# Loading Q, K and V of one batch ahead of a weight, and moving its attention steps, in a fused attention and mixer kernel

## The chip, the core and the metric

The kernel runs on one core of one Trainium2 chip. The metric is the device time of one execution in microseconds (us). Six executions of the kernel before took 321.12 to 322.65 us, with a median of 321.58. One of them was profiled: the one of 322.65 us, in which the span from the first to the last instruction is 320.9 us.

A core has five engines that run their own instruction streams in order and wait for each other through semaphores: TensorE (PE, matrix products; PEld is its weight load), VectorE (DVE), ScalarE (ACT), GpSimd (POOL) and SyncE (SP). Matrix products are written to PSUM, everything else lives in SBUF. POOL, SP and ACT also issue DMAs.

## What is computed

Eight batches, eight heads, 576 positions, 64 numbers per head; the window is 64 positions back. What comes out of the attention goes through a low-rank mix over positions (rank 32) and a two-layer perceptron of width 2048.

```python
scores = scale * np.matmul(q, k.transpose(0, 1, 3, 2))
mask = (rel >= 0) & (rel < window)
scores = np.where(mask, scores, -1000000000.0)
attn = softmax(scores)                       # written out in the reference
x = heads_side_by_side(np.matmul(attn, v))   # (8, 576, 512)
h = x.transpose(0, 2, 1) @ U @ V
u = x + h.transpose(0, 2, 1)
out = u + np.maximum(u @ w_ch1, 0.0) @ w_ch2
```

## The kernel before

The 8 x 576 = 4608 tokens are cut into nine **chunks** of 512 for the perceptron. While PE works on chunk c, the attention of batch b = c + 1 is threaded in between. The order is written out by hand. A chunk has 32 **slots** (and a last, empty one): slots 0 to 15 each make 128 columns of the hidden layer (`ch1`, L620: four matmuls psA of 128x512, then a ReLU on ACT or DVE into c1), and slots 16 to 31 each do four matmuls of the second layer (`ch2`, L648: psU, four hidden blocks for one tile of 128 tokens, a "quarter"; after the fourth quarter the sum with u goes out to HBM). After the work of a slot come the attention pieces that the tables PLACE, PLACE_1, PLACE_2 and KT_LATE (L695 to L726) put there; in chunk 0 from slot 21 on they come ahead of it. PLACE_1 is for batch 1, which runs in chunk 0.

The pieces of a batch are:

- **KT** (L232): K and Q, loaded as raw tiles kr and qr, are transposed by DVE in blocks of 32. Batches 0 to 2 take four transposes (two parts, K and Q each, 576 words of 32 bits), later batches eight (576 words of 16 bits). The eight of batch b + 1 run already in the chunk of batch b, at the slots of KT_LATE, or at PLACE["KT"] where KT_LATE has no entry.
- **S** (L347): six score pieces, run as three pairs: matmuls sc (L371), the exponential on ACT (L379) and a mask product on DVE (L386).
- **VC** (L267): V is copied into a second tile that is shifted by half a block, by DVE, ACT or POOL.
- **PV** (L394): five groups of value matmuls xr (L408). DVE then takes reciprocals (L417) and scales (L427) into xs.
- **U**, **XT**, **UP** and **V** (L437, L518, L537, L476): the low-rank mix. U makes the rank-32 product pshh and its copy hh. V makes psv (L483) in three pieces, and DVE adds xs to it, which gives u (un, L494). For batches 0 and 1, XT and UP build u transposed straight in PSUM (xT), and four copies (L551) make uTc, the operand of the first layer. For later chunks DVE transposes un into a staging tile (L570), and DMAs gather it (L596).

Two PSUM pools matter. `ps_big` has two buffers, which sc, xr, pshh, psv and xT take in turn. `mm` has three banks for psA and psU, and `tp` one bank, which only the pshh of batch 1 uses.

Before chunk 0 stands the **head** (L742 to L788): the attention of batch 0 with nothing to hide it. `turn_over` (L729) issues matmuls of zeros whose result nobody reads; they stand at places in the head, 98 of them at the start.

Loads from HBM that change the type (f32 to bf16) go through POOL's queue, in the order in which the code issues them: `load_kq` (L99), `load_v` (L123), `load_w1` and `load_w2` (L196, L199). After the head's value groups 0 and 1 that order is (L766 to L774): the second half of w1, w2 rows 0 to 7, K and Q of batch 1, w2 rows 8 to 15, V of batch 1, and U for odd batches. Then come K and Q of batch 2 and V of batch 2, and in slot 23 of chunk 0 K and Q of batch 3. V of batch 3 follows in chunk 1.

In chunk 0 the second layer runs as quarters for tokens 0 to 2 in turn (L691), and the fourth token tile has its four quarters at the end.

Of the kernel before, what the change touches and what calls it, by code (L numbers as in the profile page):

```python
# [9 lines left out]
ALU = mybir.AluOpType  # L10

BF16 = mybir.dt.bfloat16
FP32 = mybir.dt.float32
# [3 lines left out]
def kernel(  # L17
# [11 lines left out]
    nc = tc.nc  # L29
    B, H, S, D = q.shape  # L30
# [165 lines left out]
    def load_w1(lo, hi):  # L196
        nc.gpsimd.dma_start(out=w1b[:, :, lo:hi], in_=w1v[:, :, lo:hi])

    def load_w2(lo, hi):  # L199
        nc.gpsimd.dma_start(out=w2b[:, lo:hi, :], in_=w2v[:, lo:hi, :])  # L200
# [22 lines left out]
    def attention(b, alone=False):  # L223
# [213 lines left out]
        def UM(ts):  # L437
            def f():
                half = CH // 2
                if ts[0] == 0:  # L440
                    if b == 1:
                        hh["one"] = psum["tp"].tile([P, CH], FP32, name="pshh1", tag="tp")
                    else:
                        big = ps_big.tile([P, 2, CH], FP32, name="pshh", tag="big")
                        hh["one"] = big[:, 0, :]
                    if b < 2:
                        hh["ps"] = hh["one"].rearrange("p (n x) -> p n x", n=2)
                    else:
                        hh["ps"] = big[:, :, 0:half]
                ps = hh["ps"]  # L450
                for t in ts:
                    xt = x[:, t, :, :].rearrange("p h d -> p (h d)")
                    if b < 2:
                        nc.tensor.matmul(
                            hh["one"][t % 4 * R : (t % 4 + 1) * R, :],
                            ub[odd][:, t, :],
                            xt,
                            start=(t < 4),
                            stop=(t > 0),
                        )  # L460
                        continue
                    for n in range(2):
                        g = t if t < 4 else n
                        nc.tensor.matmul(
                            ps[g * R : (g + 1) * R, n, :],
                            ub[odd][:, t, :],
                            xt[:, n * half : (n + 1) * half],
                            start=(t < 4),
                            stop=(t != n),
                        )  # L470
                if ts[-1] == NT - 1:
                    hh["sb"] = wk_pool.tile([P, CH], BF16, name="hh", tag="hh")
                    nc.scalar.copy(out=hh["sb"].rearrange("p (n x) -> p n x", n=2), in_=ps)
            return f
# [133 lines left out]
    def mlp(c):  # L608
        uTc = uT_of(c)
        c1 = [None] * NFC  # L610

        psA0 = []

        def uT_cols(dc):
            cols = uTc[:, dc, :]
            if c < 2:
                return cols
            return cols.rearrange("p (i t q) -> p t i q", i=4, t=TPC)

        def ch1(i):  # L620
            def f():
                if c == 0 and i < 2:
                    if i == 0:
                        psA0.append(ps_big.tile([P, 2, CH], FP32, name="psA0", tag="big"))
                    ps = psA0[0][:, i, :]
                    todo = [(n, dc) for two in ((0, 2), (1, 3)) for n in range(2) for dc in two]
                else:
                    ps = psum["mm"].tile([P, CH], FP32, name="psA", tag="mm")[:]
                    todo = [(i, dc) for dc in range(NDC)]
                for n, dc in todo if c > 0 or i != 1 else ():  # L630
                    to = psA0[0][:, n, :] if c == 0 and n < 2 else ps
                    nc.tensor.matmul(  # L632
                        to if c < 2 else to.rearrange("p (t i q) -> p t i q", i=4, t=TPC),
                        w1b[:, dc, n * P : (n + 1) * P],
                        uT_cols(dc),
                        start=(dc == 0),
                        stop=(dc == NDC - 1),
                    )
                c1[i] = c1_pool.tile([P, CH], BF16, name=f"c1_{i}")
                if i in (DVE_RELU if c != 1 else (7, 10, 13)):  # L640
                    nc.vector.tensor_relu(out=c1[i][:], in_=ps)  # L641
                else:
                    nc.scalar.activation(out=c1[i][:], in_=ps, func=ACT.Relu)  # L643
            return f

        acc = {}

        def ch2(t, quarter):  # L648
            def f():
                g = c * TPC + t  # L650
                if c == NCH - 1 and t == TPC - 1:
                    if quarter % 2 == 0:
                        acc[t] = psum["mm"].tile([P, DM], FP32, name="psU", tag="mm")
                    cols = slice(quarter // 2 * (DM // 2), (quarter // 2 + 1) * (DM // 2))
                    for i in range(8 * (quarter % 2), 8 * (quarter % 2) + 8):
                        nc.tensor.matmul(  # L656
                            acc[t][:, cols],
                            c1[i][:, t * P : (t + 1) * P],
                            w2b[:, i, cols],
                            start=(i == 0),  # L660
                            stop=(i == NFC - 1),
                        )
                    if quarter % 2 == 1:
                        osb = out_pool.tile([P, DM], FP32, name="osb")
                        nc.vector.tensor_tensor(
                            out=osb[:, cols], in0=acc[t][:, cols], in1=u_tiles[g][:, cols], op=ALU.add
                        )
                        queue = nc.scalar if quarter == 1 else nc.sync
                        queue.dma_start(out=outf[g * P : (g + 1) * P, cols], in_=osb[:, cols])
                    return  # L670
                if quarter == 0:
                    acc[t] = psum["mm"].tile([P, DM], FP32, name="psU", tag="mm")
                for i in range(4 * quarter, 4 * quarter + 4):
                    nc.tensor.matmul(  # L674
                        acc[t][:],
                        c1[i][:, t * P : (t + 1) * P],
                        w2b[:, i, :],
                        start=(i == 0),
                        stop=(i == NFC - 1),
                    )  # L680
                if quarter == 3:
                    osb = out_pool.tile([P, DM], FP32, name="osb")
                    nc.vector.tensor_tensor(  # L683
                        out=osb[:], in0=acc[t][:], in1=u_tiles[g][:], op=ALU.add
                    )
                    nc.sync.dma_start(out=outf[g * P : (g + 1) * P, :], in_=osb[:])
            return f

        order = [(t, r) for t in range(TPC) for r in range(4)]
        if c == 0:  # L690
            order = [(t, r) for r in range(4) for t in range(3)] + [(3, r) for r in range(4)]  # L691
        return [ch1(i) for i in range(NFC)] + [ch2(t, r) for t, r in order]


# [6 lines left out]
        "V": [17, 18, 20],  # L701
    }
    PLACE_1 = {
        "KT": [11, 12, 14, 15],
        "S": [14, 14, 17, 17, 21, 21],
        "VC": [20, 21, 22, 23],
        "PV": [22, 23, 24, 25, 26],
        "U": [28],
        "XT": [28] * 4,
        "UP": [29],  # L710
    }
    PLACE_2 = {
        "V1": [0, 1, 17],
# [8 lines left out]
    KT_LATE = {  # L722
        2: [21, 22, 23, 24, 26, 27, 28, 30],
        3: [19, 20, 21, 23, 24, 26, 28, 30],
        4: [17, 18, 20, 21, 23, 25, 26, 28],
    }  # L726


    def turn_over(n, cols=CH, to=None):  # L729
        for _ in range(n):  # L730
            nc.tensor.matmul(
                (unread if to is None else to)[:, 0, 0:cols],
                idle[:, 0:P],
                idle[:, 0:cols],
                start=to is None,
                stop=to is None,
            )
# [19 lines left out]
    for f in a["VC"][0:2]:  # L757
# [6 lines left out]
    a["PV"][1]()  # L764
    a["VC"][3]()
    load_w1(1024, 2048)  # L766
    load_w2(0, 8)
    load_kq(1)
    load_w2(8, 16)
    load_v(1)  # L770
    nc.gpsimd.dma_start(out=ub[1][W:P, 0, :], in_=moe_U[0:W, :])
    nc.gpsimd.dma_start(
        out=ub[1][:, 1:NT, :], in_=moe_U[W:S, :].rearrange("(c p) r -> p c r", p=P)
    )  # L774
    xT0 = [psum["x0"].tile([P, 2, CH], FP32, name=f"xT{i}", tag="x0") for i in range(2)]
    unread = xT0[0]
    a["PV"][2]()
    a["PV"][3]()
    a["PV"][4]()
    a["XT"][0]()  # L780
    for f in a["U"]:
# [16 lines left out]
    for c in range(NCH):  # L798
# [8 lines left out]

        b = c + 1
        if b == 1:
            for f, n in zip(att[0]["V"], (6, 8, 10)):  # L810
                slots[n].append(f)
        if b < B:
            if b == 1:
# [63 lines left out]
```

## Time and profile before

| what | value |
|---|---|
| median of six executions | 321.58 us |
| the profiled execution | 322.65 us |
| its span | 320.9 us |
| PE busy | 311.0 us (97%) |
| DVE busy | 209.0 us (65%) |
| ACT busy | 106.0 us (33%) |
| POOL busy | 104.5 us (33%) |
| DMA moved | 38.05 MB, mean 119 GB/s |

The first psA matmul of each chunk in the timeline cuts the span in stages:

| stage | starts at (us) | length (us) |
|---|---|---|
| head | 0.00 | 23.96 |
| chunk 0 | 23.96 | 36.90 |
| chunk 1 | 60.86 | 34.76 |
| chunk 2 | 95.62 | 32.93 |
| chunk 3 | 128.55 | 32.93 |
| chunk 4 | 161.48 | 34.00 |
| chunk 5 | 195.48 | 33.55 |
| chunk 6 | 229.03 | 32.93 |
| chunks 7 and 8 | 261.96 | 58.96 |

How to read it. The page gives the busy time of each engine over the span, and the same in 40 slices, with the clock that PE was granted. A line of the timeline has the start, the length, the engine, the source line, the operation, what it writes and reads, how many instructions are merged in it, and in brackets how long the engine stood idle before and which instruction or landing ended that. Because engines work in order, one instruction that waits holds up all that stand behind it on its engine, also those whose operands are ready. The chain of waits goes back from the last instruction, at each step to what released it.

### The profile page before, as it was taken

The page shows a single profiled execution, that of the slowest core. Times are in us where ns is not written, and L with a number is a line of the kernel's source. Part 1 is how long each engine was busy: PE and PEld are TensorE (multiplying, and loading weights), DVE is VectorE, ACT ScalarE, POOL GpSimd, SP SyncE. Part 2 cuts the span into 40 slices and gives each one's busy share as a digit, 9 for nine tenths or more (in the row PEclk, how much of TensorE's full clock was granted, in tenths as well). Part 3 has the DMA queues.
Part 4 walks back from the last instruction along what each step waited for, and adds up shares of the span by engine and source line. Part 5 has one row for each costly group of instructions (what it writes and reads, how often), then busy time and mean ns, then how long its engine had stood idle before and what let it go on. Part 6 is the DMA issues. An engine that isn't in the chain of part 4 may idle for free.

```text
span 320.9 us, 7020 instructions
## 1 busy us (share of the span) xinstructions
PE 311.0 (97%) x2879; PEld 153.3 (48%) x2905; DVE 209.0 (65%) x368; ACT 106.0 (33%) x174; POOL 104.5 (33%) x156
## 2 busy tenths in 40 slices
PE   8889999999999999999999989999999999999995
PEld 7654444445444544454445434444444444444444
DVE  7744958778797859778967695769577722412211
ACT  1543543275008320642065204630273004203400
POOL 8681418541059303840483038503000300030000
PEclk9959999999999999999999999999999999999999
DMA  7999999999259995999599939993500140050011
GB/s 118 162 193 209 207 142 160 219 187 127 25 146 165 163 77 133 141 167 127 152 165 169 86 59 186 186 135 33 169 2 2 37 161 0 0 166 33 2 66 67
DMA packets 108929, 38.05 MB, mean 119 GB/s; under 512 B 98352, under 2 KB 101808, under 8 KB 108896
## 3 DMA queue, kind: packets, MB, share of 16 engines
q0 software_dynamic: 92480, 25.63, 106.3%
q1 hardware_dynamic: 11232, 10.69, 10.0%
q10 hardware_dynamic: 5184, 1.28, 1.8%
q8 instruction: 23, 0.38, 0.6%
q14 instruction: 10, 0.08, 0.1%
HBM read 48.94 MB, written 9.44 MB: 182 GB/s over the span
## 4 chain that ended last, share of the span: by engine, by line
PE 61%; DMA 22%; POOL 6%; DVE 5%; issue 3%; SPq 2%; DVEq 0%; POOLq 0%
PE psA L632 27%; PE psU L674 26%; DMA vA<-in_v_dram 13%; DMA qr<-in_q_dram 5%; DMA w1b<-in_moe_w_ch_dram 3%; PE xr L408 2%; SPq L596 2%; PE sc L371 2%; POOL kr L114 2%; POOL qr L114 2%; DVE un L494 2%; PE psv L483 2%; DMA uTc<-stg 1%; DVE stg L570 1%; PE psU L656 1%
## 5 line engine op out<-in xcount | busy, mean ns | idle before, releaser
L632 PE MATMUL psA<-uTc,w1b 128*128 128x512 bf16 x570 | 132.4, 380 | 0.3
L674 PE MATMUL psU<-w2b,c 128*128 128x512 bf16 x542 | 125.7, 379 | 1.2 <-issue 0.3
L643 ACT ACTIVATE c<-psA 128x512 bf16<-128x512 f32 x101 | 60.3, 597 | 170.9 <-PE psA L632 156.2
L674 PEld LDWEIGHTS <-c 128*128 128x128 bf16 x560 | 53.6, 98 | 64.5 <-issue 2.0
L632 PEld LDWEIGHTS <-w1b 128*128 128x128 bf16 x576 | 53.4, 98 | 61.2
L596 POOL DMA_DIRECT2D uTc<-stg x35 | 19.2, 557 | 114.5 <-DVE stg L570 76.1
L683 DVE TENSOR_TENSOR osb<-psU,un 128x512 f32<-128x512 f32 x35 | 23.5, 671 | 32.3 <-PE psU L674 32.2
L641 DVE TENSOR_SCALAR c<-psA 128x512 bf16<-128x512 f32 x43 | 29.5, 687 | 22.3 <-PE psA L632 20.5
L126 POOL DMA_DIRECT2D vA<-in_v_dram x32 | 28.3, 887 | 32.6 <-PE psA L632 17.6
L386 DVE TENSOR_TENSOR pts<-pts,mask 128x768 bf16<-128x768 bf16 x42 | 22.9, 556 | 18.8 <-ACT pts L379 16.5
L379 ACT ACTIVATE pts<-sc 128x768 bf16<-128x768 f32 x42 | 31.7, 810 | 3.7 <-PE sc L371 3.7
L494 DVE TENSOR_TENSOR un<-psv,xs 128x512 bf16<-128x512 f32 (+1 forms) x40 | 25.9, 674 | 9.9 <-PE psv L483 9.6
L427 DVE TENSOR_TENSOR xs<-xr,rcp 128x512 bf16<-128x512 f32 (+1 forms) x39 | 26.9, 691 | 1.3
L408 PEld LDWEIGHTS <-pts 128*64 128x64 bf16 x576 | 12.9, 111 | 12.3 <-DVE xs L427 5.3
L570 DVE STREAM_TRANSPOSE stg<-un 128x512 bf16<-128x512 bf16 x28 | 18.4, 683 | 0.0
L247 DVE STREAM_TRANSPOSE qt<-qr 128x576 bf16<-128x576 bf16 x20 | 15.8, 788 | 2.9 <-DMA qr<-in_q_dram 1.5
L408 PE MATMUL xr<-vB,pts 128*64 128x65 bf16 x320 | 15.9, 197 | 1.8 <-ACT pts L330 0.8
L114 POOL DMA_DIRECT2D kr<-in_k_dram x20 | 16.9, 847 | 1.9 <-issue 1.0
L247 DVE STREAM_TRANSPOSE kt<-kr 128x576 bf16<-128x576 bf16 x20 | 15.8, 788 | 2.7 <-DMA kr<-in_k_dram 1.9
L114 POOL DMA_DIRECT2D qr<-in_q_dram x20 | 17.0, 851 | 1.0 <-DMA vA<-in_v_dram 0.9
L371 PEld LDWEIGHTS <-kt 64*64 64x64 bf16 (+1 forms) x720 | 10.0, 105 | 9.2 <-issue 8.3
L483 PE MATMUL psv<-hh,vrep 128*128 128x512 bf16 x40 | 12.6, 379 | 1.4 <-DVE un L494 1.3
(71 smaller groups left out, 163.7 us busy)
## 6 DMA issues: line engine op xcount, KB each, us to landing
out_dram<-osb SPq DMA_DIRECT2D x35, 256.0 KB, 2.4
kr<-in_k_dram POOLq DMA_DIRECT2D x26, 288.0 KB, 10.2
qr<-in_q_dram POOLq DMA_DIRECT2D x26, 288.0 KB, 11.7
vA<-in_v_dram POOLq DMA_DIRECT2D x32, 128.0 KB, 12.8
w2b<-in_moe_w_ch_dram POOLq DMA_DIRECT2D x2, 1024.0 KB, 19.0
uTc<-stg SPq DMA_DIRECT2D x42, 32.0 KB, 2.4
uTc<-stg ACTq DMA_DIRECT2D x35, 32.0 KB, 2.4
uTc<-stg POOLq DMA_DIRECT2D x35, 32.0 KB, 2.1
```

The source lines that it names most:

```text
L114: nc.gpsimd.dma_start(out=dst[32 * part : 32 * (part + 1), off : off + NJJ * RD].rearrange("p (n x) -> p n x", x=r * D), in_=src[b, m * NJ ...
L126: nc.gpsimd.dma_start(out=va[:, t, :, 0:D], in_=v[b, :, t * P : (t + 1) * P, :].rearrange("h p d -> p h d"),)
L247: nc.vector.transpose(out=dst[:, n * S : (n + 1) * S].rearrange("q (m p e) -> q m e p", p=32, e=r), in_=src[:, 32 + n * RD : 32 + (n + 1) ...
L379: nc.scalar.activation(out=dst, in_=sc[:, :, 0 : PB * W].rearrange("p g (n w) -> p g n w", w=W), func=ACT.Exp, scale=scale,)
L408: nc.tensor.matmul(xr[r0 : r0 + W, h // 4, (h % 4) * VW : (h % 4 + 1) * VW], pts[:, g, jj * NB + blk, :], rhs, start=True, stop=True,)
L427: nc.vector.tensor_tensor(out=x[lo:hi, t, :, :].rearrange("p (a h) d -> p a h d", a=2), in0=xv[:, :, :, 0:D], in1=rcp[lo:hi].to_broadcast( ...
L494: nc.vector.tensor_tensor(out=u_tiles[g][rs, :], in0=ps[rs, n, :], in1=xt[n][rs], op=ALU.add)
L596: queues[n % 3].dma_start(out=uT_of(c)[32 * j : 32 * (j + 1), :, i * run : (i + 1) * run], in_=stages[c][32 * i : 32 * (i + 1)].rearrange( ...
L632: nc.tensor.matmul(to if c < 2 else to.rearrange("p (t i q) -> p t i q", i=4, t=TPC), w1b[:, dc, n * P : (n + 1) * P], uT_cols(dc), start= ...
L641: nc.vector.tensor_relu(out=c1[i][:], in_=ps)
L643: nc.scalar.activation(out=c1[i][:], in_=ps, func=ACT.Relu)
L674: nc.tensor.matmul(acc[t][:], c1[i][:, t * P : (t + 1) * P], w2b[:, i, :], start=(i == 0), stop=(i == NFC - 1),)
```

## The change

- **Loads.** K and Q of batch 1 are issued ahead of w2. After w2 rows 0 to 7 come U for odd batches, V of batch 1, and then w2 rows 8 to 15 as two loads of four rows.
- **Head.** A `turn_over(1)`, one 128x512 matmul of zeros, stands ahead of value groups 2, 3 and 4.
- **Chunk 0, attention of batch 1.** KT goes from slots 11, 12, 14, 15 to 7, 8, 10, 11; S from 14, 17, 21 to 10, 13, 16; VC from 20 to 23 to 16 to 19; PV from 22 to 26 to 18 to 23; U, XT and UP from 28 and 29 to 25 and 26. The V pieces of batch 0 go from slots 6, 8, 10 to 4, 6, 8. U of batch 1 takes its PSUM from `ps_big`.
- **Chunk 0, perceptron.** DVE does the ReLU of blocks 1, 5 and 14 (before: 1, 4, 7, 10 and 13). The fourth token tile accumulates in the `tp` bank, so that the second layer runs its quarters over all four token tiles in turn. For token tiles 0 and 1 the output sum is an ACT copy out of PSUM and a POOL add in place of one DVE add.
- **Transposes of later batches.** The eight transposes in the chunks of batches 4, 5 and 6 (chunks 3, 4 and 5) go to slots 19, 20, 21, 23, 24, 26, 28 and 30. Before, they stood at 17, 18, 20, 21, 23, 25, 26, 28 in the chunk of batch 4, and at PLACE["KT"] (14, 15, 16, 19, 21, 23, 25, 27) in those of batches 5 and 6.

```diff
@@ in attention(b), UM @@
                 if ts[0] == 0:
-                    if b == 1:
-                        hh["one"] = psum["tp"].tile([P, CH], FP32, name="pshh1", tag="tp")
-                    else:
-                        big = ps_big.tile([P, 2, CH], FP32, name="pshh", tag="big")
-                        hh["one"] = big[:, 0, :]
+                    big = ps_big.tile([P, 2, CH], FP32, name="pshh", tag="big")
+                    hh["one"] = big[:, 0, :]
@@ in mlp(c), ch1 @@
-                if i in (DVE_RELU if c != 1 else (7, 10, 13)):
+                if i in (DVE_RELU if c > 1 else (7, 10, 13) if c else (1, 5, 14)):
@@ in mlp(c), ch2 @@
-                if quarter == 0:
+                if quarter == 0 and c == 0 and t == 3:
+                    acc[t] = psum["tp"].tile([P, DM], FP32, name="psU3", tag="tp")
+                elif quarter == 0:
                     acc[t] = psum["mm"].tile([P, DM], FP32, name="psU", tag="mm")
...
                 if quarter == 3:
                     osb = out_pool.tile([P, DM], FP32, name="osb")
-                    nc.vector.tensor_tensor(
-                        out=osb[:], in0=acc[t][:], in1=u_tiles[g][:], op=ALU.add
-                    )
+                    if c == 0 and t < 2:
+                        nc.scalar.copy(out=osb[:], in_=acc[t][:])
+                        nc.gpsimd.tensor_tensor(
+                            out=osb[:], in0=osb[:], in1=u_tiles[g][:], op=ALU.add
+                        )
+                    else:
+                        nc.vector.tensor_tensor(
+                            out=osb[:], in0=acc[t][:], in1=u_tiles[g][:], op=ALU.add
+                        )
                     nc.sync.dma_start(out=outf[g * P : (g + 1) * P, :], in_=osb[:])
...
-            order = [(t, r) for r in range(4) for t in range(3)] + [(3, r) for r in range(4)]
+            order = [(t, r) for r in range(4) for t in range(TPC)]
@@ the tables @@
     PLACE_1 = {
-        "KT": [11, 12, 14, 15],
-        "S": [14, 14, 17, 17, 21, 21],
-        "VC": [20, 21, 22, 23],
-        "PV": [22, 23, 24, 25, 26],
-        "U": [28],
-        "XT": [28] * 4,
-        "UP": [29],
+        "KT": [7, 8, 10, 11],
+        "S": [10, 10, 13, 13, 16, 16],
+        "VC": [16, 17, 18, 19],
+        "PV": [18, 20, 21, 22, 23],
+        "U": [25],
+        "XT": [26] * 4,
+        "UP": [26],
     }
...
     KT_LATE = {
...
-        4: [17, 18, 20, 21, 23, 25, 26, 28],
+        4: [19, 20, 21, 23, 24, 26, 28, 30],
+        5: [19, 20, 21, 23, 24, 26, 28, 30],
+        6: [19, 20, 21, 23, 24, 26, 28, 30],
     }
@@ the head @@
     load_w1(1024, 2048)
+    load_kq(1)
     load_w2(0, 8)
-    load_kq(1)
-    load_w2(8, 16)
-    load_v(1)
     nc.gpsimd.dma_start(out=ub[1][W:P, 0, :], in_=moe_U[0:W, :])
     nc.gpsimd.dma_start(
         out=ub[1][:, 1:NT, :], in_=moe_U[W:S, :].rearrange("(c p) r -> p c r", p=P)
     )
+    load_v(1)
+    load_w2(8, 12)
+    load_w2(12, 16)
...
+    turn_over(1)
     a["PV"][2]()
+    turn_over(1)
     a["PV"][3]()
+    turn_over(1)
     a["PV"][4]()
@@ the loop over chunks @@
-            for f, n in zip(att[0]["V"], (6, 8, 10)):
+            for f, n in zip(att[0]["V"], (4, 6, 8)):
                 slots[n].append(f)
```

## The prediction

> **What bounds the kernel now.** I first read the page's slices: TensorE (PE) is busy in nearly every one, and its granted clock dips in one place only, the third slice (16 to 24 us).
>
> ```profile
> PE   8889999999999999999999989999999999999995
> PEclk9959999999999999999999999999999999999999
> ```
>
> So time can be won only where PE waits or runs at the lower clock. Next I cut the execution at the first psA matmul of each chunk and asked for the busy time of each stretch (columns: length, then busy time of PE, its weight loads, DVE, ACT and POOL, then clock and DMA). Chunks 2 to 6 issue almost the same PE work:
>
> ```profile
> 23.96:60.86 36.90, 36.06 (x396) 17.81 (x399) 24.63 (x43) 15.05 (x24) 16.13 (x22) 1.00 1.51 187
> ...
> 95.62:128.55 32.93, 32.82 (x294) 15.36 (x295) 26.36 (x46) 11.26 (x18) 13.72 (x20) 1.00 1.66 139
> 128.55:161.48 32.93, 32.83 (x294) 15.35 (x295) 25.99 (x45) 11.26 (x18) 15.98 (x23) 1.00 1.75 145
> 161.48:195.48 34.00, 33.00 (x294) 15.30 (x295) 25.89 (x44) 11.26 (x18) 12.92 (x20) 1.00 1.62 132
> 195.48:229.03 33.55, 33.03 (x295) 15.41 (x295) 25.80 (x44) 11.26 (x18) 12.62 (x17) 1.00 1.68 134
> ```
>
> Chunks 2 and 3 take 32.93 us each; chunk 4 takes 1.07 more and chunk 5 0.62 more. The timeline of chunk 4 on DVE and on PE shows where (start, length, engine, what, and in brackets the idle time before it with what ended it):
>
> ```profile
> 181.61 0.82 DVE L247 STREAM_TRANSPOSE qt<-qr 128x576 bf16<-128x576 bf16 x1 [1.53 <-DMA qr<-in_q_dram]
> ...
> 184.28 1.42 DVE L494 TENSOR_TENSOR un<-psv,xs 64x512 bf16<-64x512 f32 x2
> ```
> ```profile
> 185.76 0.39 PE L483 MATMUL psv<-hh,vrep 128*128 128x512 bf16 x1 [0.89 <-DVE un L494]
> ```
>
> DVE, which works in order, stands before a Q transpose until 181.61 because Q of batch 6 lands late; the adds behind it (L494) come late, and the third psv matmul waits for their PSUM buffer. Chunk 5 repeats it: DVE waits until 215.44, psv comes at 219.32.
>
> Third, chunk 0. The chain of waits goes through one load there, and PE's third group of value matmuls of batch 1 stands behind it:
>
> ```profile
> 28.31 18.82 DMA vA<-in_v_dram
> ```
> ```profile
> 49.85 0.22 PE L408 MATMUL xr<-vA,pts 128*64 128x65 bf16 x1 [0.15 <-DVE xs L427]
> ```
>
> V lands at 47.14, DVE's copies, masks and first scaling follow, and PE idles about 0.22 us before 49.85. The other stall of chunk 0 is 0.33 us in the second score pair (at 42.02, waiting for a Q transpose). So chunk 0 loses only 0.55 us beyond the 0.1 us that each change between matmul kinds takes.
>
> Last, the head, in windows of 3.41 us as the clock record cuts them:
>
> ```profile
> 13.60:17.02 3.42, 2.25 (x102) 1.77 (x86) 2.36 (x9) 3.20 (x8) 2.10 (x4) 1.00 1.55 169
> 17.02:20.43 3.41, 2.81 (x26) 1.47 (x22) 2.27 (x5) 1.31 (x6) 3.41 (x6) 0.50 1.24 180
> 20.43:23.84 3.41, 3.19 (x21) 2.31 (x21) 0.60 (x1) 1.32 (x3) 1.96 (x4) 0.50 1.12 209
> ```
>
> The clock column (third from the end) is 0.50 in two windows. PE was busy 66% of the one before them, 82% of the first, 94% of the second, after which the full clock came back.
>
> **The change, part by part.** The sum is against the profiled execution's own 322.65 us (its span 320.9 and 1.7 around it), which is the slowest of the six; their median, 321.58, is 1.07 lower. I carry the difference found there over to the median.
>
> *Late transposes in chunks 4 and 5.* The eight transposes move from slot 14 on to slot 19 on. Slot 19 begins near 183 and 217, after Q's landing at 181.6 and 215.4. Chunk 2 has this placement already and takes 32.93. So 1.07 + 0.62 = **-1.69**. Bounds: nothing, if the landing in other runs is earlier anyway, to -1.69. Chunk 3's transposes also move from 17 to 19, and as it has no excess now, that is 0. What is late next: the last transpose, at slot 30, needed by the next chunk's first scores; chunk 3's start shows no gap under that placement.
>
> *Three filler matmuls in the head (the new calls of turn_over).* Each is 128x512: 0.216 us at full clock, 0.43 at half. The first stands before the third value group, which now starts at 16.18 waiting for a DVE copy; the filler waits for an ACT exponential that ends at 16.06, so it runs about 16.12 to 16.33 and pushes the group by 0.17. The second and third fall into PE waits (16.5 and 17.1 to 17.7). Through reciprocal, scaling and the PSUM buffer the 0.17 reaches the last value group, so with the clock as now the first psA moves from 23.96 to 24.13: **+0.17**. Do they hold the clock? Two of them lie in the window 13.60 to 17.02: 2.25 + 0.43 = 2.68 of 3.42, 78%. That is nearer to the 82% that left the clock at half than to the 94% that raised it, so I take **no**. If it held: the DVE scaling that ends near 19.6 still gates the last pshh matmul, hh is ready near 20.65, four UP matmuls take 0.86 instead of 1.71, DVE's first cast starts near 21.75, and psA near 22.47: -1.49. These are both ends.
>
> The Trainium skill, page "TensorE: Matmul & The Clock Gate", section "What's actually happening", has the clock fall after a window without work and come back after one busy window; by it, 66% busy would not have cooled the clock, and the fillers would be 0.17 us of pure cost. The rows above say that it did cool; the sum goes by them.
>
> *Loads of batch 1 ahead of w2.* Each of POOL's issues here waited for the landing of the load eight issues back, so their starts read like a clock of landings:
>
> ```profile
> 28.31 0.87 POOL L126 DMA_DIRECT2D vA<-in_v_dram  x1 [4.07 <-DMA w1b<-in_moe_w_ch_dram]
> 33.38 0.88 POOL L126 DMA_DIRECT2D vA<-in_v_dram  x1 [4.20 <-DMA w2b<-in_moe_w_ch_dram]
> 34.78 0.87 POOL L126 DMA_DIRECT2D vA<-in_v_dram  x1 [0.52 <-DMA kr<-in_k_dram]
> 36.18 0.69 POOL L130 DMA_DIRECT2D vB<-in_v_dram  x1 [0.52 <-DMA qr<-in_q_dram]
> ```
>
> Loads land in order: half of w2 takes 5.07, a K or Q part 1.40. Reordered: K and Q parts at 29.7, 31.1, 32.5, 33.9; w2's first half at 39.0; V from about 41 to 45.5 (spaced as now); w2's quarters at 48.0 and 50.6. The total is unchanged, so the loads of batch 2 behind them keep their times. By "DMA: Bandwidth & Descriptors", section "Anatomy of one DMA — SWDGE (gpsimd) path", each DMA carries a fixed 2 us, which would make the split of w2's second half land at 52.6; the first use is near 57, so the sum is the same.
>
> *Chunk 0's slots.* Let T be the first psA, and a slot of four matmuls 0.863 us (28 took 6.04). Batch 0's second values-up piece (psv) starts at T + 4.31 + 0.43 + 1.73 = T + 6.47. DVE adds start 0.64 after that (30.00 to 30.64 now), and DVE then runs two adds (1.20), K transpose (1.09 to the next start), the half add (0.60), Q transpose (1.27 to the score matmul): T + 11.27. PE gets to the first score pair at T + 10.67. New stall: **+0.60**. The K transpose starts at T + 8.3, 30.8 at the earliest, against a landing at 29.7: covered. In the second pair PE waits 0.27 against 0.33 now. w2's first half is used at T + 17.7 (40.1 at the earliest) against 39.0: covered by 1.1 us, and that cover is what a late load would eat. V is wanted at T + 21.2 and later, 43.7 against 41 to 45.5 in order, with the third group at T + 23.9: covered, so the 0.22 goes. One value group fewer stands alone: about -0.1. Sum: 0.60 - 0.06 - 0.22 - 0.1 = **+0.2**. Bounds: -0.6 (no new stall) to +1.
>
> *Rest of chunk 0.* Two fewer ReLUs on DVE (0.69 each), taken by ACT (0.60 each), and two output adds replaced by ACT copies (nearest rows 0.59 and 0.60) and POOL adds, which no row shows: between nothing and, as a POOL copy of 520 columns took 0.65, some 2 us each. Behind these adds POOL issues V of batch 3, landing near 80 and read from 97: that hides them. SP's output DMAs wait for them too, and nothing waits for SP but output buffers a chunk later. The fourth accumulator in the freed PSUM bank lets w2's third quarter wait until slot 24: 0 while the loads come as above.
>
> Sum: -1.69 + 0.17 + 0.2 = -1.3. On the profiled execution 321.3; on the median 321.58 - 1.3 = **320.2**.
>
> **The rivals.**
> *Clock holds* (for it: fillers just where PE idles; against: 78%): T is 1.66 earlier than in my forecast, and chunk 0 no longer waits for V, so it passes through: 318.6.
> *The gap is the profiled run's own.* It is 1.07 above the median, and five of six are faster; if the landings of Q are earlier in them, half of the 1.69 or more isn't there to win: 321.2, no change. Against it: both chunks show it alike.
> *Slower: w2's first half gates slot 16.* It moves behind four loads (5.6 us). It decides from a landing after 41.8 (T = 24.1), where each us late is a us of PE; at 45, 321.58 - 1.3 + 3.2 = 323.5. For it: slot 16 now has w2 six us before use. Against: landings spaced evenly at 1.40 and 5.07.
>
> **How the numbers follow.** Forecast 0.45 (0.40 faster, 0.05 no change), clock holds 0.30, gap smaller 0.13, slower 0.12. 0.3% is about what a measurement of this kernel can tell from no change: faster is below 320.6, slower above 322.5. Faster 0.70, same 0.18, slower 0.12. The range takes in the clock case less 0.3 and the small-gap case plus the chunk 0 bound: 318.3 to 321.9, leaving out the slower case and tails.
>
> **What would show it.** Chunks 4 and 5 at 32.93; first psA at 24.1 with the clock at 0.50 before it (22.5 and 1.00 in the rival); the first score pair 0.6 after PE was ready; no wait for V, and none for w2 at slot 16. Wrong if chunk 0 is over 38 us, or chunks 4 and 5 keep their excess.

## The result and the profile after

The changed kernel takes 320.22 us (median of 41 executions) against 321.55 before (83): a ratio of 0.9968, with a 95% interval of 0.9958 to 0.9977, so 0.7 to 1.35 us less. The profiled execution took 320.55 us with a span of 318.8.

Stages of the changed kernel, cut at the first psA matmul of each chunk (start and end, length, busy time of PE, PEld, DVE, ACT, POOL, then clock and DMA):

```profile
0.00:23.32 23.32, 20.27 (x381) 14.99 (x385) 14.96 (x40) 8.69 (x18) 17.31 (x32) 0.93 1.37 153
23.32:60.46 37.14, 35.87 (x394) 17.89 (x399) 22.47 (x40) 17.95 (x29) 16.08 (x21) 1.00 1.62 173
...
161.08:194.01 32.93, 32.82 (x294) 15.39 (x295) 25.68 (x44) 11.26 (x18) 15.50 (x23) 1.00 1.70 140
194.01:226.95 32.94, 32.83 (x294) 15.35 (x295) 25.66 (x44) 11.26 (x18) 11.61 (x16) 1.00 1.57 138
```

Chunks 4 and 5 are down to the 32.93 us of chunks 2 and 3. Chunk 0 is 0.24 us longer than before, the head 0.64 shorter. On DVE and PE in chunk 4, no wait for Q stands ahead of the adds, and the third psv starts at 184.30 with no wait:

```profile
181.48 1.42 DVE L491 TENSOR_TENSOR un<-psv,xs 64x512 bf16<-64x512 f32 x2 [2.17 <-PE psv L480]
```
```profile
184.30 0.38 PE L480 MATMUL psv<-hh,vrep 128*128 128x512 bf16 x1
```

In chunk 0, the first score pair now waits for DVE's second transpose, as the sum said (start, length, and the wait in brackets):

```profile
32.82 0.67 DVE L491 TENSOR_TENSOR un<-psv,xs 64x512 bf16<-64x512 f32 x1
33.42 1.22 DVE L239 STREAM_TRANSPOSE qt<-qr 128x576 uint32<-128x576 uint32 x1
```
```profile
34.69 0.76 PE L371 MATMUL sc<-qt,kt 32*64 32x128 bf16 x48 [0.53 <-DVE qt L239]
```

The chain of waits has lost the 18.8 us of V. Its shares by engine, before and after:

```profile
PE 61%; DMA 22%; POOL 6%; DVE 5%; issue 3%; SPq 2%; DVEq 0%; POOLq 0%
```
```profile
PE 89%; DMA 5%; DVE 2%; issue 1%; POOL 1%; ACT 0%; POOLq 0%
```

This alone doesn't credit the new loads: the chain is at 92% PE in e1 below, which keeps the old ones. Of the DMA that is left, 9.62 us are the load of vrep in the head, for which PE waits 0.29 us:

```profile
21.83 0.81 PE L539 MATMUL xT<-vrep,hh 128*128 128x512 bf16 x3 [0.29 <-DMA vrep<-in_moe_V_dram]
```

The head's windows in the clock record show one at half, not two:

```profile
13.95:17.36 3.41, 2.08 (x70) 1.51 (x60) 1.85 (x8) 3.19 (x9) 1.74 (x4) 1.00 1.67 163
17.36:20.77 3.41, 3.41 (x36) 1.66 (x37) 2.46 (x5) 0.87 (x6) 3.41 (x7) 0.50 1.26 185
20.77:24.19 3.42, 3.07 (x29) 2.06 (x30) 1.29 (x3) 1.65 (x3) 0.98 (x2) 1.00 1.14 211
```

One profile says little of the clock, as these windows lie differently in each execution (one begins at 13.60 in the profile before, 13.95 after, 14.22 in e5 and 12.47 in e12). But each execution records its mean clock, and one half-clock window of 3.41 us in 319 takes 0.5% off it, so 1.000, 0.995 and 0.989 mean none, one and two. A half-clock stretch after the last matmul can take some 0.2% more: the profiled executions at 0.993 (after) and 0.992 (e9) each have one window in the head. So the count puts 0.992 to 0.995 down as one. It has the executions of which the clock is known, without one of the kernel before at 326.35 us and a clock of 0.979. The kernels ran on several chips, so their medians are for comparison within a row:

```
kernel                    executions with 0 / 1 / 2 or more windows    median us in each
before                     0 / 17 / 66                                     -  / 321.45 / 321.68
before + fillers           3 /  8 /  1                                 323.10 / 322.59 / 322.96
before + late              0 /  2 / 10                                     -  / 320.92 / 320.82
before + late + fillers    4 /  6 /  2                                 320.70 / 320.86 / 320.96
changed without fillers    0 /  7 / 17                                     -  / 320.25 / 321.09
changed                   15 / 27 / 18                                 319.91 / 320.19 / 321.31
```

("Late" are the late transposes.) Before, four in five executions have two windows or more; in the changed kernel three in ten. Only in the last two rows do two windows cost clearly more than one, some 0.8 to 1.1 us; a first window costs 0.3 us in the last row.

### The profile page after: what moved, and what is told of

The parts are those of the page before. It is cut to its first block, busy times and chain, and to the rows that moved or that the text cites. A ratio compares the mean times of both kernels' runs of the same rounds, so it can differ in the third digit from the quotient of the medians.

```text
span 318.8 us, 7028 instructions
## 1 busy us (share of the span) xinstructions
PE 310.1 (97%) x2880; PEld 152.9 (48%) x2908; DVE 207.0 (65%) x364; ACT 108.5 (34%) x178; POOL 108.5 (34%) x159
## 4 chain that ended last, share of the span: by engine, by line
PE 89%; DMA 5%; DVE 2%; issue 1%; POOL 1%; ACT 0%; POOLq 0%
PE psA L629 38%; PE psU L673 38%; PE xr L408 4%; PE sc L371 3%; DMA vrep<-in_moe_V_dram 3%; PE psv L480 3%; DMA qr<-in_q_dram 2%; PE psU L653 1%; PE pshh L461 1%; DVE qt L239 1%; PE xT L539 1%; DVE un L491 1%; ACT pts L379 0%; DVE kt L239 0%; PE xT L525 0%
## 5 line engine op out<-in xcount | busy, mean ns | idle before, releaser
L640 ACT ACTIVATE c<-psA 128x512 bf16<-128x512 f32 x103 | 61.5, 597 | 166.2 <-PE psA L629 166.1
L688 DVE TENSOR_TENSOR osb<-psU,un 128x512 f32<-128x512 f32 x33 | 22.1, 669 | 32.2 <-PE psU L673 32.2
L638 DVE TENSOR_SCALAR c<-psA 128x512 bf16<-128x512 f32 x41 | 28.1, 687 | 20.4 <-PE psA L629 18.8
L386 DVE TENSOR_TENSOR pts<-pts,mask 128x768 bf16<-128x768 bf16 x42 | 24.1, 582 | 18.6 <-ACT pts L379 16.2
L371 PE MATMUL sc<-qt,kt 64*64 64x128 bf16 (+3 forms) x720 | 12.9, 215 | 0.7 <-DVE qt L239 0.7
```

Source lines behind the costliest of these rows:

```text
L371: nc.tensor.matmul(sc[half * W : (half + 1) * W, g, (a - lo) * W : (z - lo) * W], operand("k", g, jj, e, kb * W, (kb + 1) * W), operand("q ...
```

## The experiments

Ratios are to the kernel before on the same chip, with their 95% intervals.

**Late transposes alone** (e1): the kernel before with

```diff
-        4: [17, 18, 20, 21, 23, 25, 26, 28],
+        4: [19, 20, 21, 23, 24, 26, 28, 30],
+        5: [19, 20, 21, 23, 24, 26, 28, 30],
+        6: [19, 20, 21, 23, 24, 26, 28, 30],
```

> The kernel before with the late transposes of batches 5, 6 and 7 alone. Theory (the waits for Q in chunks 4 and 5 are in every execution): both chunks fall to 32.93 us, and the time by 1.2 to 1.7 us (ratio 0.995 to 0.996). Rival (the two waits are the profiled execution's own): chunks at 32.93 in the profile, but the time falls by less than 0.6 us (ratio above 0.998).

0.9967 (0.9947 to 0.9987), medians 320.82 and 321.68; chunks 4 and 5 at 32.93. This is as much as the whole change gains. The waits are in ordinary executions too. Their worth is 1.06 us (0.4 to 1.7), just below the 1.2 to 1.7 that the theory expected, and less than the 1.69 read from one profile. The chain of waits, with the old loads and slots:

```profile
PE 92%; DMA 3%; POOL 2%; issue 1%; ACT 1%; DVE 1%; POOLq 0%
```

**Fillers alone** (e2): the kernel before with

```diff
+    turn_over(1)
     a["PV"][2]()
+    turn_over(1)
     a["PV"][3]()
+    turn_over(1)
     a["PV"][4]()
```

> The kernel before with the three filler matmuls in the head alone. Theory (the fillers do not hold the clock, and chunk 0 of before waits for V anyhow): within 0.4 us of before, and as many executions with a mean clock of 0.989 (two windows at half) as before has. Rival (the fillers hold or shorten the half clock): more executions at 0.995 and 1.0 than before has, first psA 0.6 to 1.5 us earlier, and still a gain of at most 0.3 us, as the third value group of batch 1 then waits for V at 49.85.

1.003 (1.0008 to 1.0052): slower, which neither theory had. The rival is right on the clock: one execution of 12 has two windows or more, where the kernel before had 26 of 35 on the same chip. The first psA came 0.92 us earlier, at 23.04. Chunk 0 gave back 0.44 of it: its value matmuls wait for V, now 0.49 us by the profile. Then chunk 4 took 35.1 us. The waits of PE in this kernel (what waited for what, us, times, longest):

```profile
PE psv L483 <- DVE un L494: 1.8, 1, 1.8
PE unread L731 <- DVE idle L142: 1.3, 1, 1.3
```

and on DVE, Q of batch 6 lands at 182.3, no earlier than in the kernel before:

```profile
182.34 0.82 DVE L247 STREAM_TRANSPOSE qt<-qr 128x576 bf16<-128x576 bf16 x1 [1.57 <-DMA qr<-in_q_dram]
```

An earlier PE only waits longer there. Why Q landed even 0.7 us later stays open: the load was issued 1.5 us later, behind a gather DMA that landed late. How the loss of 1 us in the medians comes about isn't fully shown either, as the two profiles' spans are 321.1 and 320.9.

**Late transposes and fillers** (e9), to see where that microsecond went: the kernel before with the edits of e1 and e2 together.

> The kernel before with the late transposes and the three fillers. Theory (the fillers alone were 1 us slower because an earlier chunk 4 meets a Q load that is no earlier, and this wait is now gone): as the late transposes alone, ratio 0.995 to 0.998; chunk 0 about 0.4 longer by the wait for V where the head is 0.9 shorter. Rival (the fillers cost in the head or in chunk 0 themselves): ratio 0.999 to 1.002, 0.7 us or more above the late transposes alone.

0.9969 (0.9946 to 0.9993), median 320.76. With the wait for Q gone the loss is gone: the theory stands. And with none, one or two windows the time is nearly the same (table, 320.70, 320.86 and 320.96). That would fit V's landing setting chunk 0, as in e2, but no profile of this kernel shows it. (The profiled execution, 322.34, had a long wait for Q early in the head and isn't typical.)

**Chunk 0 alone** (e3): the changed kernel without fillers and late transposes.

```diff
-        4: [19, 20, 21, 23, 24, 26, 28, 30],
-        5: [19, 20, 21, 23, 24, 26, 28, 30],
-        6: [19, 20, 21, 23, 24, 26, 28, 30],
+        4: [17, 18, 20, 21, 23, 25, 26, 28],
...
-    turn_over(1)
     a["PV"][2]()
-    turn_over(1)
     a["PV"][3]()
-    turn_over(1)
     a["PV"][4]()
```

> The changed kernel without the fillers and without the late transposes: loads, slots and perceptron of chunk 0 alone. Theory (the waits for V go, 0.6 us before the first score pair come): chunk 0 takes 37.1 us, time 0.0 to 0.4 us over before where the head's clock is alike. Rival (the reordered loads are what the change gains by): 0.7 us or more below before.

1.0009 (0.9979 to 1.0038). Chunk 0 took 37.16 us. The first psA came at 22.23, 1.7 us earlier than in the profile of before. Of this 0.8 us arrived at the end of this profile (a span of 320.1 against 320.9), and nothing in the medians (322.17 and 321.68): chunks 4 and 5 took 33.65 and 34.54, 2.3 us over 32.93, as DVE stood before Q transposes until 179.79 and 214.61. The waits of PE:

```profile
PE psv L480 <- DVE un L491: 2.0, 2, 1.4
```

**Changed without fillers** (e4, and again e11 beside the changed kernel): the last three removals of e3 alone.

> The changed kernel without the three fillers. Theory (fillers do not matter to the clock, each costs up to 0.17 us): 0 to 0.3 us below the changed kernel, that is a ratio to before of 0.995 to 0.997, and the same share of executions per number of half-clock windows. Rival (the fillers shorten the half clock): most executions at a mean clock of 0.989, 0.6 to 1.2 us above the changed kernel, ratio 0.999 to 1.000.

> The changed kernel without the three fillers once more, beside the changed kernel on the same chip. Theory (fillers shorten the half clock in most executions, and each window at half beyond the first costs about 1 us): more than half of the executions at a mean clock of 0.989, median 0.3 to 0.8 us above the changed kernel. Rival (fillers are worth nothing): within 0.2 us of it.

e4: 0.9961 (0.9939 to 0.9983). e11: 0.999 (0.9968 to 1.0011), median 321.04 where the changed kernel (e12) had 321.09. So by time the fillers' worth isn't settled: both ratios are what "worth nothing" expected, and in e11 and e12 the medians agree, since 7 of 12 executions of the changed kernel had two windows that time. That they shorten the half clock is plain in the kernel before (e2). In the changed kernel the count points the same way: none of 24 executions without fillers had no window, 15 of 60 with them did. But these are pooled over chips, and the share with two windows differs between them (11 of 42, none of 6 and 7 of 12 for the same kernel); on the one chip that ran both it is 10 of 12 against 7 of 12, which is no clear difference. An estimate from the table, 17 of 24 against 18 of 60 with two windows at about 1 us, gives some 0.4 us for the fillers, worked out and not measured.

Beside e1, which ran on the same chip, e4 also says what the loads and the work in chunk 0 are worth: medians of 320.71 with them and 320.82 without, no difference that could be told.

**The changed kernel as reference** (e5 and e12), with no edit.

> The changed kernel itself, as the reference on this chip for the other three. Both theories: ratio to before near 0.997, chunk 0 at 37.14 us, chunks 4 and 5 at 32.93. If the fillers shorten the half clock, fewer than a third of the executions at a mean clock of 0.989, where the kernel without them had 7 of 12.

> The changed kernel, as the reference for the other three on this chip: ratio to before 0.994 to 0.998, at most a third of the executions at a mean clock of 0.989.

0.9945 (0.9929 to 0.9962) and 0.9972 (0.995 to 0.9993). The profile of e5 has the clock full throughout: first psA at 21.98, chunk 0 at 37.14, time 319.24. That of e12 has two windows at half, and first psA at 24.02. The share of two-window executions was none of 6 and 7 of 12, the second above what was expected. The two profiles part after a window with almost the same PE work, first e5, then e12:

```profile
14.22:17.63 3.41, 2.49 (x56) 1.50 (x57) 2.29 (x8) 3.19 (x11) 2.34 (x4) 1.00 1.52 176
17.63:21.05 3.42, 2.86 (x32) 1.65 (x33) 1.68 (x4) 0.65 (x2) 3.42 (x7) 1.00 1.20 192
```
```profile
12.47:15.88 3.41, 2.48 (x144) 2.22 (x144) 2.91 (x10) 2.73 (x4) 1.84 (x3) 1.00 1.94 156
15.88:19.29 3.41, 3.17 (x43) 1.66 (x43) 2.26 (x7) 1.93 (x9) 3.03 (x6) 0.50 1.37 186
19.29:22.71 3.42, 3.42 (x27) 1.97 (x25) 0.97 (x3) 0.59 (x1) 2.74 (x5) 0.50 1.11 179
```

**Earlier values-up pieces** (e6):

```diff
-            for f, n in zip(att[0]["V"], (4, 6, 8)):
+            for f, n in zip(att[0]["V"], (2, 4, 6)):
```

> The changed kernel with the three values-up pieces of batch 0 at slots 2, 4 and 6 in place of 4, 6 and 8. Theory (the stall ahead of the first score pair is DVE's queue: two adds, K transpose, half add, Q transpose behind the second piece): the 0.6 us before the first score pair go to 0.1, chunk 0 takes 36.5 to 36.6, the time falls by 0.5 to 0.6 us against the changed kernel. Rival (the stall is Q's landing): it stays, and the time too.

The 0.6 us are gone: the first score pair starts without a wait.

```profile
30.96 3.62 PE L629 MATMUL psA<-uTc,w1b 128*128 128x512 bf16 x16
34.50 0.76 PE L371 MATMUL sc<-qt,kt 32*64 32x128 bf16 x48
```

So it was DVE's queue and not Q's landing. Chunk 0 took 37.06 in this profile, not 36.5, because the third score pair took 0.5 us longer (41.66 to 42.89, where it took 0.73 in the profile after), with a stop before 42.65 for which the profile names no cause; the same slots with more fillers (e10) took 36.56. Ratio 0.9935 (0.9918 to 0.9952) against the changed kernel's 0.9945 there: the gain of 0.5 us in the medians isn't certain.

**Old loads in the new slots** (e7): the changed kernel with

```diff
-    load_kq(1)
     load_w2(0, 8)
+    load_kq(1)
+    load_w2(8, 16)
+    load_v(1)
...
-    load_v(1)
-    load_w2(8, 12)
-    load_w2(12, 16)
```

> The changed kernel with the order of loads of before (w2's first half ahead of K and Q, V last). Theory (the new slots need the new order): the first score pair waits for Q's landing at 35.9 and starts at 37.2 or later, and the value groups wait for V at 45.5 to 50; chunk 0 2.5 to 4 us longer, ratio to before 1.004 to 1.009. Rival (loads do not bind): within 0.3 us of the changed kernel.

1.0084 (1.0055 to 1.0112). The score pair waits as expected, and chunk 0 takes 42.1 us, more than expected, since the wait also cost the clock. No value group waited for V, which had been expected too. PE, then its windows:

```profile
37.00 1.20 PE L371 MATMUL sc<-qt,kt 32*64 32x128 bf16 x48 [3.12 <-DVE qt L239]
```
```profile
32.53:35.94 3.41, 1.35 (x7) 0.49 (x5) 1.91 (x3) 1.23 (x3) 2.02 (x3) 1.00 1.09 206
35.94:39.36 3.42, 2.36 (x51) 1.49 (x51) 2.71 (x3) 1.47 (x2) 1.74 (x3) 0.50 1.22 207
39.36:42.77 3.41, 3.41 (x9) 1.21 (x8) 1.73 (x2) 1.24 (x3) 0.00 (x0) 0.50 1.69 187
```

PE was busy 1.35 of 3.41 us in the first, and the two windows after it ran at half.

**Old slots with the new loads** (e8): the changed kernel with

```diff
-        "KT": [7, 8, 10, 11],
-        "S": [10, 10, 13, 13, 16, 16],
+        "KT": [11, 12, 14, 15],
+        "S": [14, 14, 17, 17, 21, 21],
...
-            for f, n in zip(att[0]["V"], (4, 6, 8)):
+            for f, n in zip(att[0]["V"], (6, 8, 10)):
```

and the other rows of PLACE_1 as before too.

> The changed kernel with the attention of batch 1 and the values-up pieces of batch 0 in the slots of before; loads, fillers, accumulators and late transposes as changed. Theory (with K, Q and V landing early nothing waits in the old slots, and the 0.6 us of DVE's queue are not made): chunk 0 36.4 to 36.7 us, 0.4 to 0.7 us below the changed kernel. Rival (the earlier slots themselves win time, since the end of batch 1's chain is then far from chunk 1): 0.3 us or more above the changed kernel, with a gap at the start of chunk 1.

0.9967 (0.995 to 0.9983), median 320.58 where the changed kernel had 320.01; 0.57 us worse by medians, though the intervals overlap. Chunk 0 took 38.10 us, where 36.4 to 36.7 had been expected. My theory falls: something does wait in the old slots. It is w2, which the new order has moved behind K and Q:

```profile
39.02 1.90 PE L673 MATMUL psU<-w2b,c 128*128 128x512 bf16 x8 [0.98 <-DMA w2b<-in_moe_w_ch_dram]
```

With the old slots only one score pair stands ahead of slot 16, with the new ones two. The second takes 1.07 us of PE's time, its stall included (38.07 to 39.14 in the profile after), and the 0.6 us stall of the first pair is ahead of slot 16 too. The rival's gap at the start of chunk 1 isn't there, but chunk 1 took 0.3 us longer (35.08).

**More fillers with the earlier values-up pieces** (e10): e6 with

```diff
-    turn_over(1)
+    turn_over(3)
     a["PV"][4]()
+    turn_over(1)
```

> The version with the values-up pieces at slots 2, 4 and 6, with three fillers ahead of the last value group instead of one, and one behind it. Theory (more work in the PE wait of 17.1 to 17.7 lets the clock stay full): more than half of the executions at a mean clock of 1.0, first psA at 22.0, ratio 0.990 to 0.993. Rival (w2's first half, landing at 37.7 to 39.9, takes over as the limit when the head is short and the first score stall is gone): a wait of 0.5 to 1 us at the first psU, time as with three fillers, 0.993 to 0.995.

0.9964 (0.9943 to 0.9985), median 320.5 beside the changed kernel's 321.09. No execution of 12 had two windows, five had none, a little less than the half expected, and the ratio is above both forecasts. In the profile, at full clock all through, the first psA comes at 23.04 and not 22.0. The waits of PE name what is late then, and it is not w2 but the operand of the UP matmuls:

```profile
PE xT L539 <- DMA vrep<-in_moe_V_dram: 0.9, 1, 0.9
```

Chunk 1 also took 35.26 us, 0.5 more than in the profile after, with a stop of 0.44 us for which the profile names no cause. It is the best median of that chip, but no version here is clearly faster than the changed kernel.

## Why the prediction held, and where not

- **Late transposes.** The mechanism is shown (chunks at 32.93; e1, and e3 beside e4, which differ in them alone: 1.0009 and 0.9961). The term was mis-sized: -1.69 came from a profiled execution 1.07 above the median; alone they are worth 1.06 (0.4 to 1.7), which by e4 beside e1 is the whole gain but for some 0.1 us. The rival "the gap is the profiled run's own" was right in part.
- **Fillers.** This is the step that failed: "that is nearer to the 82% that left the clock at half than to the 94% that raised it, so I take no". The 82% is of a window that began at half clock, and says nothing of when a full clock falls. With fillers, e5 has 2.49 of 3.41 (73%) in that window and kept it, and e12, the same kernel, has 2.48 and lost it. So the busy share alone doesn't decide, and what does stays open. Nor was 2.68 of 3.42 reached: the windows lie elsewhere in each execution. In three of ten executions two windows came, as forecast (first psA at 24.02 in e12, 24.13 forecast); the "clock holds" rival came true in a quarter, with 319.91 against 321.31 for two windows: 1.4 us, not 1.66.
- **Chunk 0.** +0.2 predicted, +0.24 in the profile, stall by stall: 0.60 at the first pair (0.60 beyond the usual step), 0.33 at the second (0.27), no wait for V. The 37.1 us that this makes held in e3, e4 and e5 as well (37.14 to 37.16). The new loads and slots, which give the change its name, show no gain of their own: e3 is level with the kernel before, e4 with e1, and the changed kernel of e12 (321.09) is no faster than e9 on the same chip (320.76), which has the old loads.
- **Loads.** K and Q were put at 29.7 to 33.9 and w2 at 39.0. In the profile after, w1 itself landed 1.2 us later than before, and POOL's issues follow the landings at 30.95, 32.37, 33.75, 35.15 and 40.22, the steps being the 1.4 and 5.07 us of before. The slot 16 rival didn't come about, as some 0.7 us of w2's cover of 1.1 were left (landed by 40.22, used at 40.88); e8 shows it is real once that cover is taken away. w2's last quarter had landed by 51.44, put at 50.6 plus the same 1.2, so the split shows no cost of its own.
- **Rest of chunk 0.** It was put at nothing, and nothing shows: the POOL adds took 1.31 us each (between nothing and 2 was the estimate), and chunk 1 took 34.76 as before.
- **The sum.** Its working gives 321.58 - 1.32 = 320.26, which is 320.3 and not 320.2; the gain of 1.32 is beside a measured 1.33. That it fits so well is luck: the late transposes gain some 0.6 less than was charged, and the fillers, charged at +0.17, seem to gain some 0.4, by an estimate that no time confirms. Two errors of about the same size cancel.

What the sum did not have is that its terms are not independent; only the clock rival spoke of a wait for V that swallows an earlier start. Earlier work in the head or in chunk 0 was worth little or nothing in the kernel before (table, first row: 321.45 and 321.68; e2 and e3), as PE then waits longer for Q in chunks 4 and 5 (e2, e3), and in e2 for V in chunk 0. For Q, e9 tests it; for V alone no run does. Only with both waits gone is the head's clock clearly seen in the time (last two rows).

## What to carry to other kernels

A wait for a landing swallows whatever is won ahead of it; before adding terms, ask for each one which load stands behind it, and test parts together as well as alone. A stall read from one profile is one draw: compare that execution with the median before charging it in full. When a load is moved ahead of another, look at what uses the second one first, and put work that doesn't need it there.

## What the runs showed of the hardware

- The granted clock fell after windows in which PE was 40 to 73% busy, not only idle ones: 1.35 (e7), 2.08 (after), 2.25 (before) and 2.48 (e12) of about 3.41 us. It held after 2.49 (e5) and 2.41 (e10). The border isn't sharp: in e6 the clock stayed full after a window with 1.88.
- The Trainium skill, "TensorE: Matmul & The Clock Gate", section "What's actually happening", ties the fall to an idle window and the return to one busy window. The falls above are against the first half; for the second, one window at 3.41 of 3.41 brought the full clock back in the profile after, and one at 2.87 in e4, but not those at 2.81 (before) and 3.17 (e12).
- A wait of 3.1 us in the middle of dense matmuls (e7) cost 5 us of chunk 0 (42.14 against 37.14): 2.6 us are the wait beyond the usual 0.53, and most of the rest fell in the two windows at half clock that followed.
